# Half of a sliding-window attention's weights taken to all partitions through DRAM instead of through TensorE, on one Trainium2 core

## The chip, the core and the metric

One core of a Trainium2 chip runs the whole program in one launch. The metric is device time in microseconds (us), the median of three executions. TensorE (PE) does the matmuls, VectorE (DVE) and ScalarE (ACT) the elementwise work, GpSimd (POOL) a few small operations and part of the DMA issues, SyncE (SP) nearly all other DMA issues. The row PEclk of the profile gives the clock that was granted to PE: it is at full speed in the whole span.

## What is computed

The reference has two blocks behind each other, on 2048 positions of 1024 values in bf16:

```python
def _A_ref(x, wqkv, wo):          # 32 heads of 32, window of 8, dilation 2
    qkv = (x @ wqkv) ...
    idx = pos[:, None] - 2 * arange(8)[None, :]          # 8 offsets back
    logits = einsum('bhsd,bhswd->bhsw', q, kg) * scale   # masked where idx < 0
    attn = softmax(logits, axis=-1)
    o = einsum('bhsw,bhswd->bhsd', attn, vg)
    return o @ wo

def _B_ref(x, w_in, w_sp, b_sp, w_out):
    z = gelu(x @ w_in)
    z1, z2 = z[..., :Fh], layernorm(z[..., Fh:])
    g = einsum('ts,bsf->btf', w_sp, z2) + b_sp
    return (z1 * g) @ w_out

h  = x + _A_ref(layernorm(x), wqkv, wo)
out = h + _B_ref(layernorm(h), w_in, w_sp, b_sp, w_out)
```

So each query has only eight keys, 0, 2, ... 14 positions back. The products of queries and keys and the sum over the eight values are elementwise work, not matmuls.

## The kernel before, in words

The positions are cut into four chunks of 512 (`NCH`, `CH`), each of four row tiles of 128. A chunk c goes through these stages:

- **LN1 and QKV** (`ln1`, `qkv`, L383 to L455). The normalised x is transposed by a DMA into `xnT`; PE multiplies it with wq, wk, wv (L438); ACT copies the result out of PSUM into `stg` (L449); SP stores `stg` to `qkv_d` in DRAM (L450). A store is 256 KB in rows of 1 KB. Queries, keys and values of chunks 1 to 3 are loaded back by POOL (L469), with partition p = 4·head + j and eight values d per partition.
- **Attention, logits** (`attention`, L460 on). For each of the eight offsets w, DVE multiplies queries by shifted keys (L496, 128x4096), adds three times (L500, L503, L506), and PE sums over the four partitions of a head (`lm`, L526, a 128x32 tile), into the PSUM tile `L` whose partitions are 32·(quarter of the chunk) + head.
- **Attention, softmax** (L533 to L569). DVE takes the maximum over the offsets, subtracts, ACT takes the exponential, DVE sums and inverts, and two multiplications (L569, offsets 0 to 3, then 4 to 7) leave the weights in `attn`: 128 partitions (quarter, head), 8 offsets, 128 positions.
- **Attention, broadcast** (`pbm`, `cp`, L572 to L589). The weights are needed on the four partitions of each head, in `AB` (128 partitions, 8 offsets, 512 positions). PE does that: for each half of the offsets four matmuls with 32 rows (L581, `pb` and `pba`) against the 0/1 matrix `B4`, and four copies of 128x1024 out of PSUM per chunk and half pair (L586): for offsets 0 to 3 one on ACT and one on DVE, for offsets 4 to 7 two on ACT.
- **Attention, values** (`mul`, `dm`, `plus`, `gather`, L594 to L631). DVE multiplies the shifted values with the weights, offset by offset (L601, 128x4096): offset 0 into `av_y`, 1 into `av_z`, 2 into `av_oT`, 3 into `av_zz`, 4 into `av_b`, 5, 6, 7 into `av_p`. `av_z` is added to `av_y` and `av_zz` to `av_oT` by accumulating DMAs that POOL issues (L615, 1 MB each); the rest is added by DVE (L609), and the last addition gives `av_oT`.
- **Output projection and LN2** (`head`, L650 on). PE multiplies `av_oT` with wo (L672), DVE adds the residual (L681), ACT takes the squares (L686), POOL the root (L645). For chunks 0 to 2, ACT then normalises the four tiles in place (L714, four instructions), and one DMA transpose issued by SP (L719) gives `hnT`. Chunk 3 normalises on DVE (L698), tile by tile.
- **Gated MLP, first part** (`b_z2`, `b_z1`): PE multiplies `hnT` with w_in, the z2 half first (L745), then the z1 half (L800); ACT applies gelu (L752, L806); results go to DRAM.
- Behind the four chunks, the **second part** (L886 to L926) runs w_sp and w_out on PE, with loads only.

The order of the instructions on PE, ACT, DVE and POOL is written by hand in the sense that a small planner writes it: every operation is given to `Order.add` (L70) with an engine, a cost in us, its dependencies, a priority and a latency; `run` (L79) always picks the operation that can start first on its engine (with priorities), and the program is emitted in the order of planned starts. At run time each of these engines works through its list strictly in that order; it waits when an operand is late and never goes round it. `dma_op` (L375) enters a transfer as so many us after its dependencies, on no engine. SP's list isn't written by hand: it is put in order when the program is built, by readiness in the build's own reckoning.

The names that the prediction uses: `att_in` holds qT, kT, vT; `AB` lies in a buffer with the tag `part`; `BSLACK` (L37) is the slack in us that the planner leaves between the last multiplication of L569 and the second set of `pb` matmuls (the first set has 0.3); `last` and `abs_` are what a value multiplication `dm` waits for.

Of the kernel before, what the change touches and what calls it, by code (L numbers as in the profile page):

```python
# [11 lines left out]
BF16 = mybir.dt.bfloat16  # L12
ALU = mybir.AluOpType
ACTF = mybir.ActivationFunctionType
# [6 lines left out]
P = 128  # L21
NT = S // P
CH = 512
NCH = S // CH
TPC = CH // P
KT = D // P
DLO = 8
# [6 lines left out]
ALONE = 5  # L34
XRB = 3
LMODE = (1, 1, 1, 1)
LSLACK, BSLACK = 2.0, 2.0  # L37
Z2ACT = (4, 4, 4, 0)
PIECES = ((0, 0), (0, 4), (1, 0), (1, 4))
LNPRIO = (0, 2.0, 2.5, 2.8)  # L40
LAST_COLS = ((0, 512), (512, 896), (896, 1024))
# [21 lines left out]
class Order:  # L63
# [6 lines left out]
    def add(self, eng, us, fn, deps=(), prio=5.0, lat=0.1, take=None, free=None, table=None):  # L70
        o = _Op()
        o.eng, o.us, o.fn, o.prio, o.lat, o.free, o.table = eng, us, fn, prio, lat, free, table
        o.take = (take,) if isinstance(take, str) else take or ()
        o.deps = [d if isinstance(d, tuple) else (d, d.lat) for d in deps if d is not None]
        o.start, o.end, o.n = None, None, len(self.ops)
        self.ops.append(o)
        return o
# [49 lines left out]
def kernel(  # L127
# [13 lines left out]
    V, A, T = nc.vector, nc.scalar, nc.tensor  # L141
    dma = nc.sync.dma_start
# [6 lines left out]
    consts_d = nc.inline_tensor(_consts(), name="qt_consts")  # L149

    dpool = ctx.enter_context(tc.tile_pool(name="dram", bufs=1, space=DRAM))
    qkv_d = [dpool.tile([P, DLO, S], BF16, name=f"qkv_d{i}") for i in range(3)]
    h_d = dpool.tile([S, D], BF16, name="h_d")
    z1_d = dpool.tile([NF, P, S], BF16, name="z1_d")
    z2_d = dpool.tile([S, FH], BF16, name="z2_d")

    cpool = ctx.enter_context(tc.tile_pool(name="consts", bufs=1))
    csb = cpool.tile([P, 416], BF16, name="csb")
# [56 lines left out]
    with tc.manual_schedule(engines={mybir.EngineType.SP}):  # L215
        for i in range(TPC):
            x_slot(i)
        for i in range(2):
            for q_, lo in ((nc.sync, 0), (nc.scalar, CH)):
                q_.dma_start(xts[i][:, lo:lo + CH], x2d[i * P:(i + 1) * P, lo:lo + CH])  # L220
        for kt in range(KT):
            dma(wsb[0][:, kt, :], wq_view[:, kt, 0:D])
            if kt == 0:
                dma(csb[:], consts_d.ap()[:, :])
            if kt == 4:
                for i in (2, 3):
                    dma(xts[i], x2d[i * P:(i + 1) * P, :])
        load_pair(2)
        load_pair(3)
        dma(wsb[1][:], wq_view[:, :, D:2 * D])  # L230
        load_pair(4)
        load_pair(5)
        xl = att.tile([P, TPC, D], BF16, name="xl", tag="prod", bufs=2)
        dma(xl[:], x2d[3 * CH:4 * CH, :].rearrange("(t p) d -> p t d", p=P))
        for i in range(TPC):
            xts[3 * TPC + i] = xl[:, i, :]
        dma(wsb[2][:], wq_view[:, :, 2 * D:3 * D])
# [60 lines left out]
    att_in = {}  # L298
# [73 lines left out]
    add = o_.add  # L372
    G = {}

    def dma_op(us, fn, deps, lat=0.1, free=None):  # L375
        return add("DMA", us, fn, deps, lat=lat, free=free)
# [50 lines left out]
    def qkv(c):  # L427
        for xi in range(0 if c else 1, 3):
            wv = wsb[xi][:].rearrange("p kt (m dl) -> p kt dl m", dl=DLO)
            for dp in range(DLO // 2):  # L430
                key = ("acc", "qkv", c, xi, dp)
                deps = [G.get(("xnT", c))]
                for j, k0 in PIECES:
                    def mm(j=j, k0=k0, dl=2 * dp + j, wv=wv, key=key):
# [25 lines left out]
    def attention(c):  # L460
# [18 lines left out]
        st, parts, qs, pvs = {}, {}, [{} for _ in range(W_WIN)], {}  # L479
# [4 lines left out]
        prev = None  # L484
        for g in range(W_WIN // nw):
            adds = []
            for wi in range(nw):
                w = g * nw + wi
                o = HALO - DIL * w
# [40 lines left out]
        if c == 0:  # L530
            lms.append(add("DVE", 0.3, lambda: V.tensor_tensor(st["L"][0:32, :, 0:16], st["L"][0:32, :, 0:16], maskb, op=ALU.add),
                           lms, prio=3.0))
# [5 lines left out]
        prev = add("DVE", 1.18, mx, lms, prio=3.0, take="prod")  # L538
# [3 lines left out]
        for hw in range(2):  # L542
            ws = slice(4 * hw, 4 * hw + 4)
            def sub(ws=ws):
                V.tensor_tensor(st["sme"][:, 0, ws, :], st["L"][:, ws, :], st["m"][:].unsqueeze(1).to_broadcast([P, 4, P]), op=ALU.subtract)
            prev = add("DVE", 0.61, sub, [prev], prio=3.0, lat=0.1, free="L" if hw == 1 else None)
# [5 lines left out]
        for hw in range(2):  # L552
            prev = add("DVE", 0.34, lambda hw=hw: half(hw), [exps[hw], (prev, 0.0)], prio=3.0)
        prev = add("DVE", 0.34, lambda: V.tensor_tensor(st["ssum"][:, 0:2, :], st["ssum"][:, 0:2, :], st["ssum"][:, 2:4, :], op=ALU.add),
                   [prev], prio=3.0)
        prev = add("DVE", 0.2, lambda: V.tensor_tensor(st["ssum"][:, 0, :], st["ssum"][:, 0, :], st["ssum"][:, 1, :], op=ALU.add),
                   [prev], prio=3.0)
# [4 lines left out]
        prev = add("DVE", 0.92, rec, [prev], prio=3.0)  # L562
        abs_ = {}
        for hw in range(2):
            ws = slice(4 * hw, 4 * hw + 4)
            def at(ws=ws, hw=hw):
                if hw == 0:
                    st["AB"] = att.tile([P, W_WIN, CH], BF16, name="AB", tag="part", bufs=2)
                V.tensor_tensor(st["attn"][:, ws, :], st["sme"][:, 1, ws, :], st["rinv"][:].unsqueeze(1).to_broadcast([P, 4, P]), op=ALU.mult)  # L569
            prev = add("DVE", 0.61, at, [prev], prio=3.0, lat=0.1, take="part" if hw == 0 else None, free="prod" if hw else None)  # L570
            wait = add("DMA", BSLACK if hw else 0.3, lambda: None, [prev])
            for sh in range(2):  # L572
                def pbm(sh=sh, ws=ws, hw=hw):
                    if sh == 0:
                        pb = ps_att.tile([P, 2, 4, P], FP32, name="pb", tag="L")
                    else:
                        pb = ps_acc.tile([P, 2, 4, P], FP32, name="pba", tag="acc")
                    st["pb", hw, sh] = pb
                    for j in range(2):
                        sq = 2 * sh + j  # L580
                        T.matmul(pb[:, j], B4[32 * sq:32 * sq + 32, :], st["attn"][32 * sq:32 * sq + 32, ws, :],  # L581
                                 start=True, stop=True, tile_position=(32 * sq, 0))
                pm = add("PE", 0.20, pbm, [wait], prio=1.0, take="acc" if sh else "L", lat=0.2)
                eng = "DVE" if (hw == 0 and sh == 1) else "ACT"
                def cp(sh=sh, ws=ws, hw=hw, eng=eng):
                    (V.tensor_copy if eng == "DVE" else A.copy)(  # L586
                        st["AB"][:, ws, sh * 256:(sh + 1) * 256].rearrange("p w (j s) -> p j w s", j=2), st["pb", hw, sh][:])
                abs_[hw, sh] = add(eng, 1.25 if eng == "DVE" else 0.91, cp, [pm], prio=1.0 if eng == "ACT" else 2.9,
                                   free="acc" if sh else "L", lat=0.15)  # L589
        last = prev  # L590
        av = {}
        homes = {"y": (att, "part", 2), "z": (bp, "hn1", 1) if c < 2 else (att, "qT", 1), "zz": (bp, "hb", 1), "b": (att, "prod", 2), "p": (att, "prod", 2), "oT": (att, "oT", 1)}

        def mul(w, key):  # L594
            def f():
                if key not in av:
                    pool, tag, bufs = homes[key]
                    av[key] = pool.tile([P, DLO, CH], BF16, name="av_" + key, tag=tag, bufs=bufs)
                o = HALO - DIL * w
                abb = st["AB"][:, w, :].unsqueeze(1).to_broadcast([P, DLO, CH])  # L600
                V.tensor_tensor(av[key][:], att_in[c][2][:, :, o:o + CH], abb, op=ALU.mult)  # L601
            return f

        def dm(w, key, deps, take=None, free=None):
# [20 lines left out]
        prev = dm(4, "b", [z], take="prod")  # L625
        for w in (5, 6, 7):
            m_ = dm(w, "p", [prev], take="prod" if w == 5 else None, free="part" if w == 7 else None)
            prev = plus("b", "p", [m_], free="prod" if w == 7 else None)
        prev = plus("b", "y", [prev, g1], free="part")
        prev = plus("oT", "b", [prev, g2], free="prod", lat=0.15)  # L630
# [19 lines left out]
    def head(c):  # L650
        last = c == NCH - 1
        st = {}
        hbs = []
        prio = 4.0 + c * 0.1
        xr0 = dma_op(0.0, lambda: None, [G["attq", c]] if ("attq", c) in G else [])
        sqd = []
        for il in range(TPC):
            i = c * TPC + il
# [32 lines left out]
        if last:  # L691
            G["close"] = dma_op(0.0, close_, [G["headmm", c]] + [G["z2n", k, il] for k in range(c) for il in range(TPC)])
            for il in range(TPC):
                rs = batch_rstd(("l2", c, il), lambda il=il: st["hsum"][:, il:il + 1], lambda il=il: st["hsq"][:, il:il + 1],
                                D, f"l2_{il}", [sqd[il]], 0.5, cols=1)
# [13 lines left out]
        rs = batch_rstd(("l2", c), lambda: st["hsum"][:], lambda: st["hsq"][:], D, "l2", sqd, 0.5)  # L709
        nd = []  # L710
        for il in range(TPC):
            def nrm(il=il):
                t = G["l2", c]
                A.activation(st["hnc"][:, il, :], st["hnc"][:, il, :], ACTF.Identity, scale=t["rstd"][:, il:il + 1], bias=t["nb"][:, il:il + 1])  # L714
            nd.append(add("ACT", 1.16, nrm, [rs], prio=4.0))
        G["hdone", c] = nd[-1]
        def tr():
            hnTs[c] = bp.tile([P, TPC, KT, P], BF16, name="hnT", tag="hn%d" % (c % 2), bufs=1)
# [7 lines left out]
    def b_z2(c):  # L726
# [41 lines left out]
        for il in range(TPC):  # L768
            i = c * TPC + il
            def nrm(il=il, i=i, part=1):  # L770
                t = G["l3", c]
                z2 = st["u", il] if c < NCH - 1 else z2sb[i]
                if Z2ACT[c] > il:
                    cols = slice(part * FH // 2, (part + 1) * FH // 2)
# [3 lines left out]
                if c < NCH - 1 and part:  # L778
                    dma(z2_d[i * P:(i + 1) * P, :], z2[:])
            if Z2ACT[c] > il:  # L780
                n_ = add("ACT", 1.05, lambda f=nrm: f(part=0), [rs], prio=5.5)
# [104 lines left out]
    for c in range(NCH):  # L886
        wspT = wspTs[c]
        zg = p2.tile([P, NF, CH], BF16, name="zg", tag="zg")
        for fp in range(NF // 2):
# [3 lines left out]
            for j in range(2):  # L893
                f = 2 * fp + j
# [8 lines left out]
        for il in range(TPC):  # L903
            i = c * TPC + il
# [52 lines left out]
```

## Time and profile before

| what | us |
|---|---|
| median of 3 runs (725.95 to 726.35) | 726.03 |
| the profiled execution, its own time | 725.92 |
| its span, first to last instruction | 724.1 |
| PE busy | 719.4 |
| DVE busy | 420.1 |
| ACT busy | 227.2 |
| DMA, hardware queue of SP and ACT (q1) | 72.96 MB |
| DMA, software queue of POOL (q0) | 36.64 MB |

How to read it: the span is 1.8 us shorter than the execution's own time, since there is something ahead of the first and behind the last instruction. PE is busy nearly all the time, and so is DVE in the first 370 us. The chain of waits follows back what released what; a piece of it gives start, duration, engine, tile and line, and the count of instructions. In the timeline an instruction's duration is a little longer than the distance to the next start, because the two overlap. A DMA row of the timeline is the issue alone; the time to landing stands in the list of DMA issues. In a window of the DMA view, packets are counted per queue; a 1 KB row of a transfer is one packet.

### The profile page before, as it was taken

How to read it: one execution, taken by the hardware profiler on the slowest of the kernel's cores; microseconds unless marked ns; L12 is line 12 of the kernel's file. 1: busy time of each engine (PE TensorE's matmuls, PEld its weight loads, DVE VectorE, ACT ScalarE, POOL GpSimd, SP SyncE). 2: the span in 40 equal slices, each digit the busy share in tenths (PEclk: the TensorE clock that was granted, in tenths of full speed). 3: DMA queues.
4: the chain of work that ended last, by engine and by line, in shares of the span. 5: the costliest groups of instructions: out<-in, count | busy, mean ns of one | idle time of the engine just before them, and what ended most of it. 6: DMA issues, size and time to landing. Idle time of an engine off the chain costs nothing.

```text
span 724.1 us, 8608 instructions
## 1 busy us (share of the span) xinstructions
PE 719.4 (99%) x3553; PEld 370.4 (51%) x3553; DVE 420.1 (58%) x468; ACT 227.2 (31%) x290; POOL 50.4 (7%) x61
## 2 busy tenths in 40 slices
PE   9999999999999999999999999999999999999998
PEld 7766665666545444444444444444444444444444
DVE  6899899989999798998950102222222222222222
ACT  4423532534348866758735520000000000000000
POOL 0100010112100111001203000000000000000000
PEclk9999999999999999999999999999999999999999
DMA  9964587479983594652759999153115311120002
GB/s 327 320 186 110 186 191 190 148 221 265 285 305 59 183 195 150 232 117 47 199 147 246 262 285 300 55 143 111 38 43 136 119 37 44 34 87 11 0 19 70
DMA packets 114711, 110.51 MB, mean 153 GB/s; under 512 B 67760, under 2 KB 92240, under 8 KB 114544
## 3 DMA queue, kind: packets, MB, share of 16 engines
q1 hardware_dynamic: 105792, 72.96, 34.5%
q0 software_dynamic: 8448, 36.64, 18.4%
q8 instruction: 28, 0.46, 0.3%
q10 hardware_dynamic: 432, 0.36, 0.1%
q14 instruction: 11, 0.09, 0.0%
HBM read 55.09 MB, written 30.74 MB: 119 GB/s over the span
## 4 chain that ended last, share of the span: by engine, by line
PE 98%; DMA 1%; DVE 0%; issue 0%
PE acc L896 27%; PE acc L438 21%; PE acc L745 13%; PE acc L911 13%; PE acc L800 12%; PE acc L672 8%; PE acc L286 2%; DMA hnT<-hb 1%; PE wps L210 1%; PE pb L581 0%; PE L L526 0%; PE tpt L282 0%; PE tpa L282 0%; DVE ot L925 0%; DVE warm L207 0%
## 5 line engine op out<-in xcount | busy, mean ns | idle before, releaser
L896 PE MATMUL acc<-wspT,z2sb 128*128 128x512 bf16 x896 | 194.0, 379 | 0.0
L896 PEld LDWEIGHTS <-z2sb 128*128 128x128 bf16 x896 | 87.7, 98 | 105.7
L899 DVE TENSOR_TENSOR g<-acc,bB 128x1024 bf16<-128x1024 f32 x28 | 34.3, 1224 | 160.2 <-PE acc L896 128.1
L745 PE MATMUL acc<-win,hnT 128*128 128x512 bf16 (+1 forms) x512 | 98.2, 352 | 0.2 <-DMA hnT<-hb 0.2
L800 PE MATMUL acc<-hnT,win 128*128 128x512 bf16 x448 | 98.2, 379 | 0.0
L745 PEld LDWEIGHTS <-hnT 128*128 128x128 bf16 x512 | 49.8, 98 | 47.9 <-issue 0.7
L496 DVE TENSOR_TENSOR prod<-qT,kT 128x4096 bf16<-128x4096 bf16 x32 | 72.6, 2283 | 0.0
L911 PEld LDWEIGHTS <-zg 128*128 128x128 bf16 x462 | 44.7, 98 | 52.4
L800 PEld LDWEIGHTS <-win 128*128 128x128 bf16 x448 | 43.6, 98 | 52.6 <-issue 0.9
L918 DVE TENSOR_TENSOR ot<-acc,hr 128x1024 bf16<-128x1024 f32 x15 | 18.4, 1225 | 69.4 <-PE acc L911 69.4
L449 ACT CAST stg<-acc 128x1024 bf16<-128x1024 f32 x36 | 36.4, 1012 | 70.0 <-PE acc L438 65.0
L911 PE MATMUL acc<-wout_a,zg 128*128 128x512 bf16 (+2 forms) x264 | 58.2, 373 | 0.0
L438 PE MATMUL acc<-xnT,wk 128*128 128x512 bf16 x256 | 56.7, 380 | 0.0
L438 PE MATMUL acc<-xnT,wv 128*128 128x512 bf16 x256 | 56.3, 379 | 0.0
L672 PE MATMUL acc<-wo_sb,av_oT 128*128 128x512 bf16 x256 | 55.9, 379 | 0.0
L438 PEld LDWEIGHTS <-wv 128*128 128x128 bf16 x256 | 36.5, 143 | 18.8 <-issue 0.5
L438 PEld LDWEIGHTS <-wk 128*128 128x128 bf16 x256 | 36.4, 144 | 18.9 <-issue 0.9
L911 PE MATMUL acc<-wout_b,zg 128*128 128x512 bf16 (+2 forms) x198 | 44.4, 373 | 0.0
L438 PE MATMUL acc<-xnT,wq 128*128 128x512 bf16 x192 | 42.1, 379 | 0.0
L672 PEld LDWEIGHTS <-av_oT 128*128 128x128 bf16 x256 | 25.0, 98 | 30.1
L806 ACT ACTIVATE z1s<-acc 128x1024 bf16<-128x1024 f32 x28 | 28.6, 1022 | 33.5 <-PE acc L800 31.5
L752 ACT ACTIVATE u<-acc 128x1024 bf16<-128x1024 f32 (+1 forms) x32 | 29.3, 915 | 30.6 <-PE acc L745 30.6
(140 smaller groups left out, 585.0 us busy)
## 6 DMA issues: line engine op xcount, KB each, us to landing
qkv_d<-stg SPq DMA_DIRECT2D x36, 256.0 KB, 3.8
z_d<-z1s SPq DMA_DIRECT2D x28, 256.0 KB, 2.6
z1c<-z_d SPq DMA_DIRECT2D x28, 256.0 KB, 2.7
z_d<-u SPq DMA_DIRECT2D x12, 448.0 KB, 2.7
z2sb<-z_d POOLq DMA_DIRECT2D x12, 448.0 KB, 10.8
xr<-in_A_x_dram SPq DMA_DIRECT2D x16, 256.0 KB, 3.0
av_y<-av_z POOLq DMA_DIRECT2D x4, 1024.0 KB, 8.4
av_oT<-av_zz POOLq DMA_DIRECT2D x4, 1024.0 KB, 12.0
```

The lines of the kernel that those rows point to most:

```text
L438: T.matmul(G[key][:, j, :].rearrange("p (a b) -> p a b", a=TPC), wv[:, kt, dl, :], xnT[c][:, :, kt, :], start=(kt == 0), stop=(kt == KT - 1))
L449: A.copy(stg[:], G[key][:])
L496: V.tensor_tensor(st["prod"][:], qT[:], kT[:, :, o:o + CH], op=ALU.mult)
L672: T.matmul(st["acc", il][:, nh, :], oTs[c][:, dl, il * P:(il + 1) * P], wo_sb[:, dl, nh * CH:(nh + 1) * CH], start=(dl == 0), stop=(dl == ...
L745: T.matmul(accf[:, n0:n1], hnTs[c][:, il, kt, :], wins[hf][:, kt, n0:n1], start=(kt == 0), stop=(kt == KT - 1))
L752: A.activation(st["u", il][:, hf * 1024:hf * 1024 + wd], G["accz", c, il, hf][:].rearrange("p a b -> p (a b)")[:, 0:wd], ACTF.Gelu_apprx_t ...
L800: T.matmul(G["accy", c, fp][:, j, :].rearrange("p (a b) -> p a b", a=TPC), wt[:, kt, f0 * P:(f0 + 1) * P], hnTs[c][:, :, kt, :], start=(kt ...
L806: A.activation(z1s[:], G["accy", c, fp][:], ACTF.Gelu_apprx_tanh)
L896: T.matmul(acc[:, j, :], z2sb[a][:, f * P:(f + 1) * P], wspT[:, a, :], start=(a == 0), stop=(a == NT - 1))
L899: V.tensor_tensor(g1[:], acc[:], bB[:, c * CH:(c + 1) * CH].unsqueeze(1).to_broadcast([P, 2, CH]), op=ALU.add)
L911: T.matmul(outs, zg[:, f, il * P:(il + 1) * P], wt[:, f0, lo:hi], start=(f == 0), stop=(f == NF - 1))
L918: V.tensor_tensor(ot[:], acc[:].rearrange("p a b -> p (a b)"), hr[:], op=ALU.add)
```

## The change

Offsets 0 to 3 keep the broadcast by PE. For offsets 4 to 7 of every chunk, the four matmuls and the two copies on ACT go. In their place SP stores the half of `attn` to a DRAM tile `att_d` (128 KB) and issues four loads from it, each of which fills every fourth partition of `AB` (j, j+4, ...) with all four quarters: 32 partitions by four rows of 1 KB. The planner enters all five as one transfer of 7.0 us. In `AB` the offsets 4 to 7 now lie as (quarter, offset, position), so the value multiplications of these offsets read the weights in runs of 128 with three free dimensions, and write through such a view too. `BSLACK`, now 0.3, is used for the first half alone, which had 0.3 before.

Two more edits: of chunk 2's four LN2 normalisations, two go from ACT to DVE (planned at 0.5 us each, priority 0.6), in the form that chunk 3 has; and the load of the constants goes from SP's queue, behind the first part of wq, to ACT's queue, behind the two loads that stand there.

```diff
-LSLACK, BSLACK = 2.0, 2.0
+LSLACK, BSLACK = 2.0, 0.3
+L2DVE = (0, 0, 2)
...
+    att_d = [dpool.tile([P, CH], BF16, name=f"att_d{i}") for i in range(NCH)]
...
+        A.dma_start(csb[:], consts_d.ap()[:, :])
         for kt in range(KT):
             dma(wsb[0][:, kt, :], wq_view[:, kt, 0:D])
-            if kt == 0:
-                dma(csb[:], consts_d.ap()[:, :])
...
             prev = add("DVE", 0.61, at, [prev], prio=3.0, lat=0.1, take="part" if hw == 0 else None, free="prod" if hw else None)
-            wait = add("DMA", BSLACK if hw else 0.3, lambda: None, [prev])
+            if hw:
+                def spread(ws=ws):
+                    dma(att_d[c][:], st["attn"][:, ws, :].rearrange("p w s -> p (w s)"))
+                    for j in range(4):
+                        dma(st["AB"][j::4, 4:8, :], att_d[c][:].rearrange("(q h) n -> h q n", h=32))
+                abs_[1, 0] = abs_[1, 1] = dma_op(7.0, spread, [prev])
+                break
+            wait = add("DMA", BSLACK, lambda: None, [prev])
...
-                abb = st["AB"][:, w, :].unsqueeze(1).to_broadcast([P, DLO, CH])
-                V.tensor_tensor(av[key][:], att_in[c][2][:, :, o:o + CH], abb, op=ALU.mult)
+                vs = att_in[c][2][:, :, o:o + CH]
+                if w < 4:
+                    V.tensor_tensor(av[key][:], vs, st["AB"][:, w, :].unsqueeze(1).to_broadcast([P, DLO, CH]), op=ALU.mult)
+                else:
+                    abb = st["AB"][:, 4:8, (w - 4) * P:(w - 3) * P].unsqueeze(1).to_broadcast([P, DLO, 4, P])
+                    V.tensor_tensor(av[key][:].rearrange("p d (q s) -> p d q s", q=4), vs.rearrange("p d (q s) -> p d q s", q=4), abb, op=ALU.mult)
...
-                A.activation(st["hnc"][:, il, :], st["hnc"][:, il, :], ACTF.Identity, scale=t["rstd"][:, il:il + 1], bias=t["nb"][:, il:il + 1])
-            nd.append(add("ACT", 1.16, nrm, [rs], prio=4.0))
+                if il < L2DVE[c]:
+                    V.tensor_scalar(st["hnc"][:, il, :], st["hnc"][:, il, :], t["nmean"][:, il:il + 1], t["rstd"][:, il:il + 1],
+                                    op0=ALU.add, op1=ALU.mult)
+                else:
+                    A.activation(st["hnc"][:, il, :], st["hnc"][:, il, :], ACTF.Identity, scale=t["rstd"][:, il:il + 1], bias=t["nb"][:, il:il + 1])
+            nd.append(add("DVE", 0.5, nrm, [rs], prio=0.6) if il < L2DVE[c] else add("ACT", 1.16, nrm, [rs], prio=4.0))
```

## The prediction

> **What bounds the kernel now.** I read the busy shares first, then the digits by slices, then the chain of waits, and last the timeline of one chunk. The page has:
>
> ```profile
> PE 719.4 (99%) x3553; PEld 370.4 (51%) x3553; DVE 420.1 (58%) x468; ACT 227.2 (31%) x290; POOL 50.4 (7%) x61
> DVE  6899899989999798998950102222222222222222
> ```
>
> PE is the bound: what takes work off PE shows up in the time unless PE then waits for something. The second line tells for what: in the first 20 slices (370 us) DVE is nearly as full as PE, with little room to catch up. So I need the price of the removed matmuls, the slack of DVE behind PE, and the arrival of the new transfer. The chain of waits, whose columns are start, duration and piece, runs on PE:
>
> ```profile
> 85.71 0.32 PE pb L581 x2
> ...
> 86.04 30.37 PE acc L438 x140
> 116.41 13.81 PE acc L672 x64
> ...
> 167.66 0.32 PE pb L581 x2
> ...
> 192.31 5.40 PE acc L745 x28
> 197.72 13.81 PE acc L672 x64
> ...
> 251.28 0.32 PE pb L581 x2
> 251.61 4.42 PE acc L800 x20
> ...
> 406.57 24.17 PE acc L800 x112
> ```
>
> The last row gives a matmul on undisturbed PE: 24.17/112 = 0.216 us. The first block removed, with the 140 matmuls behind it, lasts 116.41 − 85.71 = 30.70 us, of which the 140 account for 30.21: the block costs PE **0.49**. Likewise chunk 1: 192.31 − 167.66 = 24.65, less 24.17: **0.48**; chunk 2: 256.03 − 251.28 = 4.75 less 20 x 0.216: **0.43**; chunk 3 is taken as chunk 2. Sum 1.83 us. The blocks are short because the four run side by side with others; that is all PE can win here.
>
> **The change part by part.**
>
> *Matmuls and copies.* PE −1.83 us at most. The two copies per chunk on ACT are worth nothing: ACT is 31% busy and nobody waits for it behind these. The L586 copy on DVE belongs to the first half and stays.
>
> *Store and four loads: when do the weights arrive?* In chunk 1 the timeline (start, duration, engine, instruction) has:
>
> ```profile
> 163.06 1.29 DVE L569 TENSOR_TENSOR attn<-sme,rinv 128x512 bf16<-128x512 f32 x2
> 164.02 0.88 POOL L368 DMA_DIRECT2D win<-in_B_w_in_dram  x1 [8.61 <-PE acc L438]
> 171.37 1.23 POOL L615 DMA_DIRECT2D av_y<-av_z  x1 [6.47 <-DVE av_z L601]
> 175.13 2.28 DVE L601 TENSOR_TENSOR av_b<-vT,AB 128x4096 bf16<-128x4096 bf16 x1
> 193.60 2.29 DVE L609 TENSOR_TENSOR av_oT<-av_oT,av_b 128x4096 bf16<-128x4096 bf16 x1
> ```
>
> The second half of the weights is ready at 163.06 + 1.29 = 164.35; its first user, offset 4 (`av_b`), starts at 175.13. The new way has 10.8 us, and store and loads follow each other. How long they take depends on who shares the DMA engines: the first load of `win` (1.5 MB, POOL's queue) and then the accumulating `av_y` run in just this stretch. Three windows, of 168 to 171, 172.5 to 173 and 173 to 179 us, count packets per queue (packets, MB, share; the first also lists the stores issued in it, with us to landing):
>
> ```profile
> q0 software_dynamic: 244, 1.00, 81.2%
> q1 hardware_dynamic: 244, 0.25, 23.1%
> ...
> qkv_d<-stg SPq DMA_DIRECT2D x1, 256.0 KB, 4.9
> ```
> ```profile
> q1 hardware_dynamic: 163, 0.16, 90.1%
> ```
> ```profile
> q0 software_dynamic: 256, 1.05, 98.6%
> ```
>
> With POOL's queue running, SP's queue gets one 1 KB packet for one of POOL's 4 KB: 244/3 = 81 per us under the load of `win`; 256/6 = 42 is POOL's own rate under the gather, and I take SP's share as one to one again. Alone, between the two, SP's queue does 163/0.5 = 326 per us. The page shows what such a store costs when nobody is in the way:
>
> ```profile
> z_d<-z1s SPq DMA_DIRECT2D x28, 256.0 KB, 2.6
> ```
>
> 256 packets alone are 0.8 us of these 2.6, so 1.8 lie around the data; I put 1.4 of them behind the last packet. Now chunk 1: `att_d` (128 packets) goes out at about 164.5, under the `win` load, and lands near 170. The `qkv_d` store that ACT finishes just behind (256 packets) stands ahead of the four loads (512). These 768 go: from 168 to 172.5 at 81 per us, 365; 0.5 us alone until the gather's first packets, 163; the other 240 at 42 per us, 5.7 us, to 178.7; with 1.4, landed at **180.1**. `av_b` was due at 175.13: DVE waits S = 5.0 us.
>
> Queued behind the waiting `av_b` on DVE is everything that leads to `av_oT`, whose last addition ends at 193.60 + 2.29 = 195.89, then 200.9. PE would begin the projection (L672) at 197.72 − 0.48 = 197.24: it idles 3.7 us. Its slack was 197.24 − 195.89 = 1.35 us, so PE waits from S = 1.35 on, and the change as a whole breaks even with S near 3.4. On SP's list the next `qkv_d` stores stand behind the loads, which wait for the landing of `att_d`; ACT, and then PE, only notice when SP stands still for longer than four `xn`/`stg` buffers last; I take 0. The four loads are 1.4 us of issuing on SP, at the 0.36 of such a row, within the above:
>
> ```profile
> 257.17 0.36 SPq L807 DMA_DIRECT2D z_d<-z1s  x1
> ```
>
> Chunk 0:
>
> ```profile
> 81.43 1.29 DVE L569 TENSOR_TENSOR attn<-sme,rinv 128x512 bf16<-128x512 f32 x2
> ...
> 90.31 1.26 POOL L615 DMA_DIRECT2D av_y<-av_z  x1 [6.43 <-DVE av_z L601]
> ...
> 94.05 2.28 DVE L601 TENSOR_TENSOR av_b<-vT,AB 128x4096 bf16<-128x4096 bf16 x1
> ...
> 112.53 2.29 DVE L609 TENSOR_TENSOR av_oT<-av_oT,av_b 128x4096 bf16<-128x4096 bf16 x1
> ```
>
> ```profile
> q1 hardware_dynamic: 1, 0.00, 0.0%
> ```
>
> Ready at 82.72, due at 94.05. The gather's packets begin some 1.7 us behind its issue, as in chunk 1 (171.37, and 173), at 92.0, and the window of 90.7 to 91.9, the last fence, has one packet: the engines have nothing to do. 768 packets at 326 per us are 2.4 us; between 88.5 and 91.9 they fit, and with 1.4 land by 93.3: no wait. If the store stands behind one more `qkv_d` store, the loads meet the gather and land near 99: a wait of 5, against a slack at L672 of 116.41 − 114.82 = 1.6.
>
> Chunks 2 and 3:
>
> ```profile
> 247.14 1.29 DVE L569 TENSOR_TENSOR attn<-sme,rinv 128x512 bf16<-128x512 f32 x2
> ...
> 259.12 2.28 DVE L601 TENSOR_TENSOR av_b<-vT,AB 128x4096 bf16<-128x4096 bf16 x1
> ```
>
> 10.7 us again between 248.43 and 259.12, but without a `win` load ahead; two transfers of 2.6 and four issues of 0.36 end at about 255. No wait in 2, and none in 3, where there is no QKV stage beside it.
>
> *The multiplications in runs of 128.* Sixteen of L601 at 2.28 us get a different pattern; no row has it. Nearest are the reads in runs of 128 and in one piece:
>
> ```profile
> L586 DVE CAST AB<-pba 128x1024 bf16<-128x1024 f32 x4 | 4.9, 1225 | 3.7 <-PE pba L581 3.7
> ```
> ```profile
> L899 DVE TENSOR_TENSOR g<-acc,bB 128x1024 bf16<-128x1024 f32 x28 | 34.3, 1224 | 160.2 <-PE acc L896 128.1
> ```
>
> The former writes in runs of 128, the latter in one piece, and they cost the same; I take 0, and nothing less, since the number of values is the same. Upper end: if the multiplication fell to that rate (4 x 1.224 = 4.9), 2.6 each, 42 us in all.
>
> *LN2 of chunk 2.* The timeline and the chain:
>
> ```profile
> 305.38 2.36 ACT L714 ACTIVATE hb<-hb,l2nb,l2rstd 128x1024 bf16<-128x1024 bf16 x2
> 308.83 2.36 ACT L714 ACTIVATE hb<-hb,l2nb,l2rstd 128x1024 bf16<-128x1024 bf16 x2
> 318.46 3.63 PE L745 MATMUL acc<-win,hnT 128*128 128x512 bf16 x16 [0.23 <-DMA hnT<-hb]
> ```
> ```profile
> 311.22 7.20 DMA hnT<-hb
> ```
> ```profile
> L698 DVE TENSOR_SCALAR hb<-hb,l_0nmean,l_0rstd 128x1024 bf16<-128x1024 bf16 x1 | 0.5, 542 | 0.0
> ```
>
> ACT's four end at 311.19 and the transpose of 7.20 lands at 318.42, when PE has waited 0.23 us. With two on DVE, ACT's other two end at 307.74 and the transpose comes up to 3.4 us earlier: PE gains **0.23**, and what it saved before this point isn't lost here, which it would be otherwise. The 2 x 0.54 us that DVE gets lie in its chain of chunk 3; PE has the 128 matmuls of z2 ready meanwhile: 0, upper end +1.1; below nothing there is no reason to expect.
>
> *The constants.* Before:
>
> ```profile
> 2.13 0.43 SPq L224 DMA_DIRECT2D csb<-qt_consts  x1
> ...
> 6.06 0.39 PEld L282 LDWEIGHTS <-xn 128*128 128x128 bf16 x4 [0.90 <-DVE xn L271]
> ```
>
> PE's first use of them is at 6.06, held by LN1 (`xn`). On ACT's queue the issue moves half a microsecond earlier, and wq's parts move up by 0.43 on SP: 0, within 0.1 either way.
>
> *Sum*, against the profiled execution: 725.92 − 0.97 (two blocks) + 3.7 (chunk 1) − 0.86 (two blocks) − 0.23 = 727.56; the execution is 0.11 under the median of 726.03, so **727.7**.
>
> *The skill's rule.* The Trainium skill, page "DMA: Bandwidth & Descriptors", section "Anatomy of one DMA — SWDGE (gpsimd) path", gives a transfer as about 2.0 us plus its bytes over 436 GB/s; for software queues, but nothing in it depends on a neighbour. By it, as an estimate, store and loads (2.3 and 3.2) end 5.5 us after 164.35, long before `av_b`. The trace agrees where queues are empty (256 KB by it 2.6; the page 2.6) and not where POOL's queue runs (4.9 us is the median for such a store in the window of 168 to 171).
>
> **The rivals.**
>
> *The loads land in time everywhere.* For it: 10.8 us against two quiet transfers of 2.6 and four issues of 0.36, 6.6 in all; SP may also run the loads ahead of the `qkv_d` store (256 packets fewer: the last are then gone before the gather begins at 173, and landed at 174.4). Against it: the equal counts of 168 to 171. It decides below a landing at 176.5 (S = 1.35), where PE has nothing to wait for; the change as a whole wins below 178.5. Then 725.92 − 1.83 − 0.23 + 0.11 = 724.0. The skill's rule above gives this one.
>
> *Chunk 0 waits as well.* The store of its weights or the loads stand behind one more `qkv_d` store, and fall under the gather from 92.0: S = 5, less the slack 1.6 and the 0.49, hence +3.4 to +4 on the forecast: about 732. Against: DMA is free just before 92.0. This is the slow end, decided by whether the last load packet leaves before or behind the gather's first.
>
> *The loads go one after another.* If each waits for the one before (they fill one tile), a load is 2.6 or more and under the gather 5: chunk 1 till 187, S = 12, and chunk 2 late by about 1.4: about 737. Against: they write different partitions.
>
> *DVE takes the new pattern slowly.* 16 x up to 2.6, up to 768. Against: the two rows of L586 and L899.
>
> **How the numbers follow.** Forecast (own range 726.5 to 728.9, from landing 1.2 us either way) 0.44; loads in time 0.30; chunk 0 too 0.18; one after another 0.05; slow pattern 0.03. About 0.2%, 1.45 us, is what a measurement of this kernel tells from no change: faster is under 724.6, slower over 727.5. The loads in time give faster, 0.30; of the forecast's own range the lower part (S of 3.4 to 4.8) is the same, 0.17; the rest is slower, 0.53. The range holds the first three cases: 723.4 (724.0 less 0.6 for smaller parts) to 732.5.
>
> **What the profile after would show.** L581 with 16 matmuls in place of 32 and PE's sum 1.8 lower. The forecast is right if in chunk 1 `av_b` starts after an idle of 4 to 6 us on DVE, put down to the load of `AB`, and L672 behind it after 3 to 5 us of idle PE, put down to `av_oT`, with no such pair in chunks 0, 2 and 3. It is wrong if `av_b` has no idle time (the loads were ahead of the store, or got more than a packet for a packet), or if chunk 0 shows one too. The row of L745 behind `hnT` should have no wait. L601 at 2.28 for `av_p` and `av_b` says that the pattern is free; any other mean moves the time by 16 times the difference.

## The result and the profile after

The changed kernel takes **723.46 us** (median of 8, 723.34 to 725.48) where the kernel before took 725.95 in the same series: a ratio of 0.997, 95% interval 0.9961 to 0.998. The forecast was 727.7, slower; what came is the first rival, priced at 724.0: the loads are there almost in time. The profiled execution took 723.34, its span is 721.6. The page's busy line:

```profile
PE 714.1 (99%) x3493; PEld 370.3 (51%) x3537; DVE 420.8 (58%) x470; ACT 217.7 (30%) x280; POOL 51.2 (7%) x61
```

PE's count fell by 60 where 16 matmuls went, so 44 records are missing here and its busy sum can't be compared. The chain of waits can, with one piece of before that the prediction did not need:

```profile
23.23 51.80 PE acc L438 x240
```

and of the changed kernel (L439 is the old L438, L684 the old L672, L816 the old L800):

```profile
23.23 51.80 PE acc L439 x240
...
115.92 0.22 PE acc L684
...
164.10 0.32 PE pb L589 x2
...
196.75 4.97 PE acc L684 x23
...
404.33 24.17 PE acc L816 x112
```

The start is the same; the projection of chunk 0 begins 0.49 earlier (116.41 before), that of chunk 1 0.97 earlier (197.72), and the 112 matmuls of z1 2.24 earlier (406.57). From there the two programs run alike; the last 0.25 of the 2.5 us that the span lost lies behind the last matmul and isn't explained by any part of the change. I use the distance from the 240 to the 112 matmuls as a ruler below: 383.34 before, 381.10 after.

Now the place where the forecast lost its 3.7 us, the timeline of chunk 1:

```profile
163.90 0.33 SPq L574 DMA_DIRECT2D att_d<-attn  x1
164.36 0.36 SPq L451 DMA_DIRECT2D qkv_d<-stg  x1
...
166.00 2.69 SPq L576 DMA_DIRECT2D AB<-att_d  x4
...
175.53 2.29 DVE L613 TENSOR_TENSOR av_b<-vT,AB 128x4096 bf16<-128x4096 bf16 x1 [0.80 <-DMA AB<-att_d]
```

The issues of the window of 160 to 170 us, with KB and us to landing:

```profile
AB<-att_d SPq DMA_DIRECT2D x4, 128.0 KB, 7.7
att_d<-attn SPq DMA_DIRECT2D x1, 128.0 KB, 2.0
```

The store lands 2.0 us behind its issue, at 165.9, not near 170. SP has all four loads out by 168.7, and the last lands at 175.4. VectorE waits 0.80 us, where 5.0 were forecast, and PE's projection has no wait at all. How the loads got through is seen in the window of 173 to 174:

```profile
q1 hardware_dynamic: 333, 0.31, 91.4%
q0 software_dynamic: 19, 0.05, 14.6%
```

While the load of `win` runs out and before the gather gets going, SP's queue has the engines nearly to itself for more than a microsecond, where the forecast gave it half a microsecond: it sends 445 packets between 172.5 and 174. Ahead of that the forecast's count was right: 378 packets from 168 to 172.5, where it had 365.

The row of the first matmul on chunk 2's `hnT` has lost its wait, and the new read pattern costs VectorE nothing (by-form groups; 2.28 before):

```profile
316.67 1.68 PE L761 MATMUL acc<-win,hnT 128*128 128x512 bf16 x6
```
```profile
L613 DVE TENSOR_TENSOR av_p<-vT,AB 128x4096 bf16<-128x4096 bf16 x12 | 27.5, 2290 | 0.3
L613 DVE TENSOR_TENSOR av_b<-vT,AB 128x4096 bf16<-128x4096 bf16 x4 | 9.1, 2287 | 0.8 <-DMA AB<-att_d 0.8
```

The second row also says that chunk 1 is the only one where `av_b` waits.

### The profile page after: what moved, and what is told of

Its sections match the earlier page's. It is cut to its first block, busy times and chain, and to the rows that moved or that the text cites. A ratio compares the mean times of both kernels' runs of the same rounds, so it can differ in the third digit from the quotient of the medians.

```text
span 721.6 us, 8559 instructions
## 1 busy us (share of the span) xinstructions
PE 714.1 (99%) x3493; PEld 370.3 (51%) x3537; DVE 420.8 (58%) x470; ACT 217.7 (30%) x280; POOL 51.2 (7%) x61
## 4 chain that ended last, share of the span: by engine, by line
PE 98%; DMA 0%; DVE 0%; issue 0%; ACT 0%
PE acc L912 27%; PE acc L439 21%; PE acc L816 13%; PE acc L761 13%; PE acc L927 13%; PE acc L684 8%; PE acc L287 2%; DMA xp<-in_A_x_dram 0%; PE L L527 0%; PE tpt L283 0%; PE pb L589 0%; DVE bnst L242 0%; DVE xn L272 0%; DVE bnst L243 0%; PE tpa L283 0%
## 5 line engine op out<-in xcount | busy, mean ns | idle before, releaser
L816 PE MATMUL acc<-hnT,win 128*128 128x512 bf16 x448 | 98.0, 379 | 0.0
L816 PEld LDWEIGHTS <-win 128*128 128x128 bf16 x448 | 43.7, 98 | 52.6 <-issue 0.7
L439 PE MATMUL acc<-xnT,wk 128*128 128x512 bf16 x256 | 56.5, 380 | 0.0
L439 PE MATMUL acc<-xnT,wv 128*128 128x512 bf16 x256 | 56.1, 380 | 0.0
L684 PE MATMUL acc<-wo_sb,av_oT 128*128 128x512 bf16 x250 | 55.6, 379 | 0.3
L439 PEld LDWEIGHTS <-wv 128*128 128x128 bf16 x256 | 36.7, 144 | 18.5 <-issue 0.2
L439 PEld LDWEIGHTS <-wk 128*128 128x128 bf16 x256 | 36.6, 144 | 18.7 <-issue 0.7
L439 PE MATMUL acc<-xnT,wq 128*128 128x512 bf16 x192 | 42.1, 380 | 0.0
L684 PEld LDWEIGHTS <-av_oT 128*128 128x128 bf16 x256 | 25.0, 98 | 30.1
L501 DVE TENSOR_TENSOR prod<-prod 128x2048 bf16<-128x2048 bf16 x32 | 38.4, 1217 | 0.1
```

Source lines behind the costliest of these rows:

```text
L439: T.matmul(G[key][:, j, :].rearrange("p (a b) -> p a b", a=TPC), wv[:, kt, dl, :], xnT[c][:, :, kt, :], start=(kt == 0), stop=(kt == KT - 1))
L501: V.tensor_tensor(dst, p_[:, 0:4, :], p_[:, 4:8, :], op=ALU.add)
L684: T.matmul(st["acc", il][:, nh, :], oTs[c][:, dl, il * P:(il + 1) * P], wo_sb[:, dl, nh * CH:(nh + 1) * CH], start=(dl == 0), stop=(dl == ...
L816: T.matmul(G["accy", c, fp][:, j, :].rearrange("p (a b) -> p a b", a=TPC), wt[:, kt, f0 * P:(f0 + 1) * P], hnTs[c][:, :, kt, :], start=(kt ...
```

## The experiments

Theory: the parts bring the removed blocks and the gap ahead of `hnT`; a late `av_b` costs nothing until the slack at the projection is used up; and what puts the loads on the right side is that the store left before the packets of `win` began. Rivals stand in the expectations. All times are medians, with the ratio to the kernel before on the same chip. "Ruler" is the stretch defined above, in the profiled execution; it leaves out what happens in the first 23 us.

| kernel | time | ratio, 95% interval | start of the 240 | ruler |
|---|---|---|---|---|
| before | 725.95 | | 23.23 | 383.34 |
| changed | 723.46 | 0.997, 0.9961 to 0.998 | 23.23 | 381.10 |
| LN2 alone | 725.66 | 0.9995, 0.9986 to 1.0004 | 23.35 | 382.93 |
| spread without LN2 | 725.20 | 0.9987, 0.9978 to 0.9996 | 23.52 | 382.71 |
| chunk 1 by PE | 724.15 | 0.9974, 0.9964 to 0.9984 | 23.93 | 381.60 |
| store late | 738.96 | 1.0181, 1.0167 to 1.0195 | 23.64 | 395.75 |
| constants back on SP | 723.56 | 0.9967, 0.9955 to 0.998 | 23.52 | 381.11 |
| constants alone on ACT | 726.23 | 1.0008, 0.9999 to 1.0017 | 23.74 | 383.28 |
| 1 transfer more, 8 KB packets | 724.21 | 0.9981, 0.9972 to 0.999 | 25.80 | 381.10 |
| 2 of them | 723.58 | 0.9975, 0.9966 to 0.9984 | 23.35 | 381.10 |
| 1 transfer more, 1 KB rows | 723.92 | 0.997, 0.9957 to 0.9983 | 23.87 | 381.11 |
| 2 of them | 723.52 | 0.9964, 0.9952 to 0.9977 | 23.68 | 381.11 |
| 4 of them | 730.36 | 1.0058, 1.0043 to 1.0073 | 23.86 | 387.31 |
| win late | 729.30 | 1.0047, 1.0032 to 1.0062 | 23.61 | 386.49 |

**LN2 alone**, the kernel before with

```diff
+L2DVE = (0, 0, 2)
...
+                if il < L2DVE[c]:
+                    V.tensor_scalar(...)
...
```

> The kernel before with the two LN2 normalisations of chunk 2 on VectorE and nothing else. Theory: PE's start-to-start gap ahead of the first matmul on hnT of chunk 2 is 0.39 us longer than between two other matmuls, and this goes: 725.95 - 0.39 = 725.6, with no wait row in front of that matmul. Rival, what PE gains there is lost again later because VectorE got 1.1 us more work: 725.95 or a little above.

The median is where the theory had it, but its interval doesn't exclude no change. The ruler does: 383.34 − 382.93 = 0.41, the 0.39 of PE's start-to-start gap.

**Spread without LN2**, the changed kernel with

```diff
-L2DVE = (0, 0, 2)
+L2DVE = (0, 0, 0)
```

> The changed kernel with all four LN2 normalisations of chunk 2 on ScalarE again, the spread and the load of the constants as changed. Theory, the parts add up: 723.46 + 0.39 = 723.9, and the wait ahead of the first matmul on hnT of chunk 2 is back. Rival, the spread needs the faster LN2 to keep its gain, since a later stage would take it back: 724.5 to 725.

The rival was right and the parts don't add up. 0.41 and 383.34 − 382.71 = 0.63 make 1.04, and together they give 2.24. The chain and the timeline of this kernel show why:

```profile
23.52 51.80 PE acc L439 x240
...
310.11 8.40 DMA hnT<-hb
...
406.23 24.17 PE acc L816 x112
```
```profile
318.56 2.76 PE L761 MATMUL acc<-win,hnT 128*128 128x512 bf16 x12 [1.43 <-DMA hnT<-hb]
```

The transpose starts 1.11 us earlier than before (311.22), since the blocks of three chunks are gone; but it lasts 8.40 instead of 7.20 and lands where it did. PE waits 1.43 us and has given back 1.2 of the 1.4 that it had saved. In the changed kernel the transpose starts at 306.36, 4.86 us earlier than before, and any of these durations would have done. So in these programs the second edit isn't an extra of 0.4: it carries about 1.6 of the gain. Most of that hangs on the 8.40: with the 6.7 of most transposes here (last section), this one would have landed at 316.8, ahead of the 317.13 at which PE began to wait for it.

**Chunk 1 by PE**: the changed kernel, with the old broadcast in chunk 1 alone.

```diff
+SPREAD = (1, 0, 1, 1)
...
-            if hw:
+            if hw and SPREAD[c]:
...
-            wait = add("DMA", BSLACK, lambda: None, [prev])
+            wait = add("DMA", 2.0 if hw else BSLACK, lambda: None, [prev])
...
-                if w < 4:
+                if w < 4 or not SPREAD[c]:
```

> The changed kernel with chunk 1 broadcast by PE as before; chunks 0, 2 and 3 are spread through DRAM. Theory, the wait of 0.8 us of VectorE in front of av_b in chunk 1 costs nothing because it is under the slack of 1.35 us at the projection: the spread of chunk 1 is worth its block of 0.48, so 723.46 + 0.48 = 723.9. Rival, the wait costs what it lasts: 723.46 + 0.48 - 0.80 = 723.1, faster than the changed kernel.

The ruler is 0.50 longer than the changed kernel's (381.60 against 381.10), which is the block of 0.48 and nothing for the wait; the rival asked for 0.3 shorter. A wait of 0.80 on VectorE is free here. The median, 0.26% under before, can't tell the two apart by itself: in the profiled execution the 240 matmuls alone start 0.7 us later than in the changed kernel's.

**Store late**: in chunk 1 ScalarE copies the weights onto themselves before SP stores them, which puts the store behind one `qkv_d` store.

```diff
+                src = prev
+                if c == 1:
+                    def again(ws=ws):
+                        A.copy(st["attn"][:, ws, :], st["attn"][:, ws, :])
+                    src = add("ACT", 0.6, again, [add("DMA", 1.0, lambda: None, [prev])], prio=1.0)
-                abs_[1, 0] = abs_[1, 1] = dma_op(7.0, spread, [prev])
+                abs_[1, 0] = abs_[1, 1] = dma_op(7.0, spread, [src])
```

> The changed kernel, but in chunk 1 the store of the weights waits for a copy of them onto themselves by ScalarE, so that it leaves about 2 us later and behind one qkv_d store, when the load of win already has packets running. Theory, it is the early landing of the store (165.92, ahead of the packets of win) that decided: now it lands near 172.5, the loads start there and share with the gather packet for packet (about 45 per us), and land near 188 to 190; av_b waits 13 to 15 us, PE idles that less 1.35 ahead of the projection, and the time is about 736 (731 to 740). Rival, a load takes its 7.5 us whoever else runs: landing near 178.4, a wait of 3.8 and 725.9.

Its timeline, and behind it the landing of the store (the list of issues, KB and us):

```profile
166.44 0.33 SPq L574 DMA_DIRECT2D att_d<-attn  x1
...
173.51 4.75 SPq L576 DMA_DIRECT2D AB<-att_d  x4
...
189.16 2.29 DVE L618 TENSOR_TENSOR av_b<-vT,AB 128x4096 bf16<-128x4096 bf16 x1 [14.02 <-DMA AB<-att_d]
...
194.12 6.35 PE L439 MATMUL acc<-xnT,wv 128*128 128x512 bf16 x16 [5.81 <-ACT stg L450]
...
209.99 2.31 PE L689 MATMUL acc<-wo_sb,av_oT 128*128 128x512 bf16 x5 [4.11 <-DVE av_oT L626]
```
```profile
att_d<-attn SPq DMA_DIRECT2D x1, 128.0 KB, 7.0
```

2.5 us later at the source are 13.6 us later at the loads. The store now takes 7.0 us and lands at 173.5; the loads go out into the gather, the last lands at 189.0, as the theory said, and `av_b` waits 14.02. The price comes in two waits of PE: behind ScalarE's copies, whose buffers SP's list had not emptied (the other price that the prediction named and put at 0), then at the projection. They are 9.9 us of the 14.65 that the ruler grew by; most of the rest is told in the last section. The rival's 725.9 is far off.

**Constants back on SP** (the changed kernel with the edit below) and **constants alone on ACT** (the kernel before with the reverse edit):

```diff
-        A.dma_start(csb[:], consts_d.ap()[:, :])
         for kt in range(KT):
             dma(wsb[0][:, kt, :], wq_view[:, kt, 0:D])
+            if kt == 0:
+                dma(csb[:], consts_d.ap()[:, :])
```

> The changed kernel with the load of the constants on SP's queue again, behind the first part of wq. Theory: on ACT's queue the constants share the engines with wq and land at 6.2 to 6.9 us, and PE's first use of them starts 0.2 to 0.9 us late, of which 0 to 0.7 is left at the end; on SP's queue they land near 5.4 to 5.7 and the wait goes. About 0.3 under the changed kernel: 723.1, or 2.9 under the kernel before. Rival, the prediction's own term (0, within 0.1): 723.4.

> The kernel before with the load of the constants on ACT's queue and nothing else. Theory: the constants land a us later and PE starts 0.2 to 0.9 us late: 0.3 above the kernel before in the median, with more scatter. Rival, the prediction's own term: within 0.1 of the kernel before.

By the medians this is inconclusive: they lean both ways by 0.1 to 0.3, within their intervals; the ruler doesn't move, as it must be. On ACT's queue the constants landed at 5.8 to 7.5 us in the eleven executions profiled, on SP's at 5.35 to 5.72 in three, though they are issued half a microsecond earlier; in eight of the eleven PE's first use waits for them, 0.6 to 1.9 us. The start of the 240 matmuls is 23.2 to 23.5 in the three profiled executions with the constants on SP and 23.2 to 25.8 in the others.

The 25.8 shows a second price that the medians hide. It is an execution of the kernel with one more transfer in 8 KB packets (below), and its chain begins:

```profile
1.65 5.81 DMA csb<-qt_consts
...
8.33 3.12 PE acc L289 x32
...
25.80 51.80 PE acc L441 x240
```

PE waits 1.7 us for the constants; then its granted clock is 0.62 between 8 and 12 us, and 32 matmuls that take 2.10 us in the kernel with one transfer of 1 KB rows take 3.12. This execution took 725.83, 1.6 over its kernel's median, with a mean clock of 0.998 over the span. Of the 70 executions of the kernels that have the constants on ACT and no long wait of PE further on, nine have such a clock, the changed kernel's 725.48 among them, and lie 1.4 to 2.5 us above their kernel's median; of the 79 with the constants on SP for which a clock is on record, none. So this edit costs about 2 us in one execution of eight; that the wait is the cause in the other eight of the nine, which have no profile, is argued from this agreement.

**Transfers in between** (four kernels): in chunk 1, one or two more copies of the 128 KB, DRAM to DRAM, between store and loads; then one, two and four of them into a tile twice as wide, so that their rows can't be joined (the diff is that of two).

```diff
+    att_x = dpool.tile([P, 2 * CH], BF16, name="att_x")
+    att_y = dpool.tile([P, 2 * CH], BF16, name="att_y")
...
+                    for n_ in range(2 if c == 1 else 0):
+                        dma((att_x, att_y)[n_ // 2][:, (n_ % 2) * CH:(n_ % 2 + 1) * CH], att_d[c][:])
                     for j in range(4):
```

> The changed kernel, with one more transfer of 128 KB (the stored weights read and written to a DRAM tile that nobody uses) between store and loads in chunk 1. Theory: 144 more packets stand ahead of the last load, at 45 per us beside the gather: it lands 3.2 us later, near 178.6, av_b waits 4.0 instead of 0.8, and PE idles 4.0 - 1.35 = 2.65 ahead of the projection: 723.46 + 2.65 = 726.1 (725.4 to 726.8). Rival, the slack at the projection is wider than 1.35 or the load does not queue: 723.5 to 724.

> As the one before with two such transfers. Theory: 288 packets, landing 6.4 us later near 181.8, av_b waits 7.2, PE idles 5.85: 723.46 + 5.85 = 729.3 (728.3 to 730.3); the step from one transfer to two is the full 3.2. If SP's list then holds up the next qkv_d stores long enough, a wait of PE behind ScalarE's copies shows too. Rival, the slack is wider or the load does not queue: 724 to 725.

These two failed as doses: each copy went as 16 packets of 8 KB, not 128 of 1 KB. The last load landed 0.3 us later with 256 KB more ahead of it, and the ruler stayed at 381.10.

> As dup1, but the additional transfer of 128 KB goes into rows of 1 KB that don't lie together, so that it is 128 packets of 1 KB instead of 16 of 8 KB. Theory, the queue shares by packets, not by bytes: 144 more packets ahead of the last load, at about 45 per us beside the gather, landing near 178 instead of 175.4; av_b waits 3.4, PE idles about 2 ahead of the projection: 725.5 (724.8 to 726.5). Rival, the landing isn't set by the queue (dup1 and dup2 moved it by 0.3 or less): 723.5.

> Two such transfers in rows of 1 KB: 288 packets, landing near 181, av_b waits 6.5, PE idles about 5.2: 728.7 (727.5 to 730). Rival: 723.5.

> Four of them: 576 packets, landing near 187.5, av_b waits 13, PE idles about 11.5 in all (a part of it may show ahead of the QKV matmuls, where ScalarE's copies wait for SP's list, as in the kernel with the late store): 735 (732 to 739). Rival: 724.

With one and two copies the theory's arithmetic fell: 144 and 288 more packets ahead of the last load moved its landing to 175.8 and 175.7, not to 178 and 181 (these executions had begun 0.6 and 0.4 later, too). The window of 173 to 175 us of the kernel with two, and the issue of the gather in the changed kernel and in this one:

```profile
q1 hardware_dynamic: 766, 0.70, 101.5%
q0 software_dynamic: 23, 0.05, 6.3%
```
```profile
170.88 1.23 POOL L627 DMA_DIRECT2D av_y<-av_z  x1 [6.46 <-issue]
```
```profile
171.33 1.23 POOL L631 DMA_DIRECT2D av_y<-av_z  x1 [6.46 <-issue]
```

For two whole microseconds POOL's queue hardly moves, although the gather was issued at 171.3. From the gather's issue to its first packets it is 3.8 us here, 3.1 in the changed kernel and 1.8 in the kernel before, with chunk 1 on PE, and with the late store, whose loads are not out by then. So in these runs the gather starts later when SP's queue has packets waiting, and later still when it has more; why it does isn't shown. Everything that is queued before this hole ends gets through at over 300 packets per us. Up to two copies, what matters is to be queued in time, not how much there is.

Four copies show the other side. SP's timeline, then the waits:

```profile
170.00 3.42 SPq L580 DMA_DIRECT2D AB<-att_d  x4
...
180.89 2.29 DVE L617 TENSOR_TENSOR av_b<-vT,AB 128x4096 bf16<-128x4096 bf16 x1 [5.53 <-DMA AB<-att_d]
...
201.73 10.49 PE L688 MATMUL acc<-wo_sb,av_oT 128*128 128x512 bf16 x40 [4.34 <-DVE av_oT L625]
```

Three loads go out at 170.0 to 171.4 and land by 176.6. The fourth is issued only at 172.84: SP's wait is put down to the `qkv_d` store of 165.00, the eighth transfer ahead of this load, which lands at 172.83. (The next issue, at 174.01, waits for the eighth transfer ahead of it in the same way.) It misses the hole and lands at 180.87. This is nearly the case that the prediction described (landing at 180.1, a wait of 5.0, PE idle 3.7), and it has nearly the price: a wait of 5.53, PE idle 4.34, hence a slack of 1.19 where the prediction read 1.35. The time was 730.36, below the 735 expected, since of all the volume only the one late load mattered; and 1.9 us more than the idle time went (387.31 − 381.10 = 6.2), of which the last section tells. The first three loads also say something on the forecast: they go out when it had them go out, behind a store that lands near 170, and they are in time.

**Win late**: in the planner the load of `win` also waits for the loads of `AB`, which puts it behind the gather `av_y` on POOL's list.

```diff
-                abs_[1, 0] = abs_[1, 1] = dma_op(7.0, spread, [prev])
+                abs_[1, 0] = abs_[1, 1] = G["spread", c] = dma_op(7.0, spread, [prev])
...
+        if c == 1:
+            G["win", 0].deps.append((G["spread", 1], 0.0))
```

> The changed kernel with the load of win in chunk 1 issued behind the gather av_y instead of ahead of it, so that no queue of POOL runs beside store and loads. Theory: the loads land near 171, av_b has no wait, and the time stays at 723.5, since a wait of 0.8 was under the slack. Rival, the 0.8 us cost something: 722.7. Second rival, the landing isn't set by the shared queue: landing near 175.4 as before.

The issues of the window of 166 to 169 us, and PE's new wait:

```profile
AB<-att_d SPq DMA_DIRECT2D x4, 128.0 KB, 2.5
```
```profile
199.00 3.52 PE L761 MATMUL acc<-win,hnT 128*128 128x512 bf16 x12 [3.81 <-DMA win<-in_B_w_in_dram]
```

The first half of the theory held: alone, a load takes 2.5 us instead of 7.7, the last lands at 170.7, and `av_b` doesn't wait. The time did not stay: the load of `win` that was moved pushed its second part to 198.95, PE ran out of weights for 3.81 us, and the run is slower than before. So the 0.8 us were not worth buying, and the run says nothing about their price; that is shown by the kernel with chunk 1 on PE. None of the runs beats the changed kernel by more than the medians scatter.

## Why the prediction was wrong

- **Right: the blocks.** 0.49, 0.48 and 0.43 were read from the chain, and chunk 3 was taken as chunk 2; with the gap of 0.39 at `hnT` they make 2.2, and the ruler lost 2.24.
- **Right: the shape of the question.** The copies on ScalarE, the pattern in runs of 128 (2.287 and 2.290) and chunks 0, 2 and 3 cost nothing; chunk 1 is the only one with a wait, it is put down to the load of `AB`, and the slack is about 1.35: 0.80 stays free, 5.53 costs 4.34.
- **Right: one packet for one packet** while `win` is loaded: 81 of SP's and 81 of POOL's in the microsecond of 169 to 170 in the changed kernel.
- **Wrong, and the cause of the wrong sign: the landing of the loads in chunk 1**, 180.1 by the prediction (179.6 with the 0.49 that chunk 0 had saved), 175.4 by the trace. Two terms were mis-sized, and the second decides. First, "`att_d` goes out at about 164.5, under the `win` load, and lands near 170": the `win` load had been issued, but its packets hardly ran yet, and the store slipped through in 2.0 us; 2.5 later and behind one more store it took 7.0. I had taken the issue of a POOL transfer for the start of its traffic, though the trace of before has the first packets of `win` 1.6 us behind its issue and the bulk of them near 167. By itself this would not have made the wait: the three loads that went out at 170.0 to 171.4 in the kernel with four copies landed by 176.6, 1.2 us later than here in an execution that had begun 0.6 later. Second, "0.5 us alone until the gather's first packets": that hole was read from before, where SP's queue had little to send. With loads waiting in it, the gather itself starts later, and the hole is 1 to 2 us long at over 300 packets per us. From 172.5 to 174 the sum had some 205 packets (163, and a microsecond at 42), the trace has 445: the 240 more are above the 198 that the sum still had to send at 174.
- **Wrong in size: LN2.** The 0.23 is the row of the wait; start to start it was 0.39 (the ruler of LN2 alone: 0.41). The sentence that without this edit PE's earlier savings would be lost at that place came true by luck: the transpose moved up with PE (310.11 against 311.22), and the 1.2 us were lost because it took 8.40, which the prediction did not foresee.
- **Missed: the tail of the constants.** In the medians "0, within 0.1" is neither confirmed nor refuted; but nine of 70 executions are about 2 us longer, and none of the 79 with the constants on SP.
- **Slips that changed nothing.** The first load of `win` is 2 MB by the list of issues, not 1.5; no sum uses its size. For chunk 0 the slack of 1.6 shrinks by the 0.49, so the wait of PE would be 5 − 1.1 = 3.9, within the 3.4 to 4 that stand there, though the words subtract the 0.49.

By chances, the rival that came had 0.30, and the rule of the page "DMA: Bandwidth & Descriptors" of the Trainium skill that went with it gave the right outcome by a sum that isn't what happened: the 5.5 us estimated from it for store and loads were 11.5 here (163.9 to 175.4), and 6.3 in chunk 3 (330.5 to 336.9), where nothing else ran.

## What to carry to other kernels

Where a new transfer meets others, find out which packets are already running when it is issued, not which transfers have been issued: here a store that left 1.5 us before a long load's first packets took 2 us, and one that left within them, behind another store, 7. A wait is free up to the slack of the engine that ends last, so price the slack first and then ask only on which side of it the new wait falls; a landing time that decides the sign deserves a range that is centred on neither side. And an edit that removes a small wait further down can be what lets savings ahead of it survive, so such parts are to be tested together and apart.

## What the runs showed of the hardware

**A long wait of PE costs more than it lasts.** Behind the 4.34 us of idle PE in the kernel with four copies, the windows (PE, PEld, DVE, ACT, POOL busy, granted clock, DMA share, GB/s) read:

```profile
201.70:203.00 1.30, 1.27 (x4) 0.53 (x5) 1.30 (x1) 0.00 (x0) 0.00 (x0) 0.61 1.02 404
203.00:205.50 2.50, 2.50 (x7) 0.90 (x6) 2.50 (x2) 0.00 (x0) 0.00 (x0) 0.52 1.05 419
205.50:208.00 2.50, 2.50 (x14) 1.12 (x12) 1.50 (x2) 0.00 (x0) 0.00 (x0) 1.00 1.03 379
```

In these rows the clock is below full for 2 · (1.30 · 0.39 + 2.50 · 0.48) = 3.4 us, if it is at half all that time, and a matmul takes 0.427 us instead of 0.216. The projection's 64 matmuls take 15.67 us in the chain instead of 13.81, so 1.9 us are lost on top. The same stands behind the waits of the kernels with the late store and the late `win`. It means that my price for a wait of 3.7 was too low by nearly 2. The Trainium skill, page "TensorE: Matmul & The Clock Gate", section "What's actually happening", tells of a half-rate state after an idle window of about 3.4 us and of full rate after as long a busy one; by that, the trace agrees in the factor and in the 3.4 us. It differs in one thing: in the execution with the late constants a wait of 1.7 us was enough, in a stretch (5 to 8 us) in which PE was busy for 1.28 of 3 us.

**A DMA transpose with an instruction load beside it ends later.** The issues and queues of the stretch from issue to landing, of the spread without LN2 and of the changed kernel:

```profile
q8 instruction: 1, 0.02, 0.7%
...
hnT<-hb SPq DMA_TRANSPOSE x1, 8.4
```
```profile
hnT<-hb SPq DMA_TRANSPOSE x1, 6.7
```

Over the runs here, 38 transposes to the `hnT` of chunks 0 to 2 with no packet of the instruction queue beside them took 6.66 to 6.75 us; the four with a packet of 16 KB beside them took 7.06, 7.20, 8.40 and 8.54, all four of them the transposes of chunk 2. That the packet is the cause is argued from this agreement; no run took it away.
